# Maxima over the partitions taken by two TensorE products instead of a GpSimd reduction, and a mask and an identity built by VectorE

## The chip, the cores and the metric

The kernel runs on one core of a Trainium2 chip. What counts is the device time of one execution, in microseconds (us). The engines are named as the profile names them: PE is TensorE (PEld its weight loads), DVE is VectorE, ACT is ScalarE, POOL is GpSimd, SP is SyncE, which issues the DMAs. Each engine runs its own instructions in one fixed order; between engines they wait on semaphores.

## The reference

Attention over 2 batches and 8 heads of 576 tokens with 64 features each, then two dense stages over 1152 tokens of 512 features:

```
out_d  = softmax(scale * q_d k_d^T) v_d        # q_d, k_d, v_d: means over 4 neighbouring tokens
attn   = softmax(where(|i - j| < 4, scale * q k^T, -1e9)) v
x      = repeat(out_d, 4) + attn
x      = (silu(x @ w_gate) * (x @ w_val)) @ w_out                 # d_ff 1536
logits = x @ w_gate2;  P = exp(logits - max);  8 rounds of row and column normalization
out    = sum over 8 experts of P[:, e] * (relu(x @ w1[e]) @ w2[e])   # d_ff 1024
```

Inputs and outputs are float32, except that the three weights of the first dense stage come as float64.

## The kernel before, in words

**Three stages.** The attention works on 8 pairs of heads (2 batches, 4 pairs each). For each head `scores` makes the banded products (`s`, with the mask added by a product of the bf16 identity `identb` and the bf16 mask `maskb`) and the pooled ones, DVE takes row maxima (`stm`) and their scaled negatives (`nb`), ACT the exponentials (`ex`), DVE the reciprocal of the sums (`rs`), and POOL multiplies them in. `turn` transposes the result on PE with the float32 identity `ident` (`t`, copied to `at`), `combine` multiplies by v (`o`) and makes x1 from two averages (`x`), which is split into two float16 halves (`xhl`) with one scale for all of x1. POOL also pools q and v (`qt`, `qd`, `vt`, `vdz`). Four heads are started ahead (`AHEAD`).

The first dense stage (MoE 1) multiplies these halves by gate and value weights. `prep_gv(f)` loads a column block f as float64 words (`rawg`), converts it on ACT and DVE (`cvg`, five passes), takes the largest magnitude of each partition (`mxg`), then **the maximum over the partitions**, makes a power of two of it (`pow2`: `u`, `s`, `i`), and splits the block into halves (`gv`). The twelve blocks are numbered 0 to 11; blocks 0 to 4 are prepared while the attention still runs, and the products of blocks 0 to 2 on the first 512 tokens (24 each, in the two PSUM banks of tag `y`) lie between those of the attention. After the attention come the other blocks, w_out, and the second dense stage (MoE 2), 8 experts with Winograd's form of Strassen's products.

**The maximum over the partitions** is `allmax`, used 34 times: once for x1's scale (`g_v`, of a sum of products `vv` of v with itself), 12 times for the gate and value blocks (`g_gv`), twice each for `g_a` and `g_x`, once for the logits (`g_lg`) and 16 times for the experts' weights (`g_w`).

**Order.** A scheduler writes every engine's order from the program text and a timeline of its own; queues then run in that order. Where an instruction waits, everything behind it on its engine waits too.

**Constants.** POOL sets the mask and the identity with its affine_select; ACT makes bf16 copies; DVE clears three halves of `qz` (q of two heads, each padded with zeros), POOL the fourth and the pads of `vz` and `vdz`.

An instruction named ISA in POOL's order stands for a change of the code that POOL has loaded or for a custom instruction; a custom one has an output and an input behind it.

Of the kernel before, what the change touches and what calls it, by code (L numbers as in the profile page):

```python
# [36 lines left out]
HI_MIN = 2.0 ** -15  # L37
NEG = -1.0e9
# [11 lines left out]
NWARM = 5  # L50
QDV = (0, 1, 2)
# [4 lines left out]
def tile_kernel(ctx, tc, qT, kT, vw, vd4, va, wgv, wo, wg2, w1, w2, out):  # L56
    nc = tc.nc
# [18 lines left out]
    # products of zeros while the first loads run, so that the tensor engine's clock is up  # L76
# [10 lines left out]
    V.memset(qz[0][64:, 0], 0.0)  # L87
    V.memset(qz[0][:64, 1], 0.0)
    V.memset(qz[1][64:, 0], 0.0)
# [3 lines left out]
    for i in range(2):  # L93
# [3 lines left out]
    mask = ap.tile([P, P], F32, tag="mask", bufs=1, name="mask")  # L97
    G.memset(mask, 0.0)
    G.affine_select(out=mask, in_=mask, compare_op=ALU.is_ge, fill=NEG, base=FAC - 1,
                    pattern=[[-1, P]], channel_multiplier=1)  # L100
    band = G.affine_select(out=mask, in_=mask, compare_op=ALU.is_ge, fill=NEG, base=FAC - 1,
                    pattern=[[1, P]], channel_multiplier=-1)
    with tc.issue_after(band.ins):
        ident = ap.tile([P, P], F32, tag="ident", bufs=1, name="ident")
        make_identity(nc, ident)
        identb = ap.tile([P, P], BF16, tag="identb", bufs=1, name="identb")
        A.copy(identb, ident)
        maskb = ap.tile([P, 4, P], BF16, tag="maskb", bufs=1, name="maskb")
        A.copy(maskb, mask[:, None, :].to_broadcast([P, 4, P]))
        G.memset(qz[1][:64, 1], 0.0)  # L110
        for i in range(2):
            G.memset(vz[i][:, :, 0, 64:], 0.0)
            G.memset(vz[i][:, :, 1, :64], 0.0)
            G.memset(vdz[i][:, :, 0, 64:], 0.0)
            G.memset(vdz[i][:, :, 1, :64], 0.0)
        ones = cp.tile([P, P], F32, name="ones")
        G.memset(ones, 1.0)
# [20 lines left out]
    def allmax(mx, n, nm):  # L138
        g = tmp(n, f"g_{nm}")
        G.partition_all_reduce(g, mx, channels=P, reduce_op=RED.max)  # L140
        return g
# [41 lines left out]
    def prep_gv(f):  # L183
        """A column block of w_gate and of w_val."""
        w = wp.tile([P, 7 * 4 * P], F16, tag="wA", bufs=WB, name=f"gv{f}")
        w = w[:, :4 * DM].rearrange("p (a n) -> p a n", a=2)
        src = load_f64(wgv[f], f"g{f}", f >= NX)
        mx = tmp(1, f"mxg{f}")
        A.activation(w[:, 0], src, AF.Abs, accum_out=mx)
        s, gv_inv[f] = pow2(allmax(mx, 1, f"gv{f}"), 1, f"gv{f}")  # L190
        split(w[:, 0], w[:, 1], src, s)
        gv_w[f] = w
# [4 lines left out]
    def prep_wo(i):  # L197
        """Two row blocks of w_out, each row with its own scale."""
# [13 lines left out]
    def prep_w1(e):  # L212
        """The left operands of the seven products, of one column block of each half at a time."""
        r = []
# [7 lines left out]
        m = tmp(1, f"mw1{e}")  # L222
        V.tensor_reduce(m, allmax(mx, 4, f"w1{e}"), axis=AX.X, op=ALU.max)
        s, inv = pow2(m, 1, f"w1{e}", room=4.0)
# [25 lines left out]
    def prep_w2(e):  # L250
# [10 lines left out]
        m = tmp(1, f"mw2{e}")  # L261
        V.tensor_reduce(m, allmax(mx, 4, f"w2{e}"), axis=AX.X, op=ALU.max)
        s, inv = pow2(m, 1, f"w2{e}")
# [37 lines left out]
    def x1_scale():  # L301
        """x1 is the sum of two averages of v, whose largest square lies below the largest entry of a sum of
        Gram matrices; the high halves of the words of v are bfloat16s, close enough for a bound."""
# [10 lines left out]
        V.tensor_scalar(m.bitcast(U32), allmax(mx, 1, "v").bitcast(U32), 0x7F800000, 1, op0=ALU.bitwise_and,  # L314
# [4 lines left out]
    def attention():  # L319
        """Generator: the pieces of the attention, of two heads at a time."""  # L320
# [153 lines left out]
    def gv_step(c, f, early):  # L474
# [17 lines left out]
        if early:  # L492
            # silu(g) = g (1 + tanh(g / 2)) / 2, in the table that holds exp
# [28 lines left out]
    ia = {}  # L522

    def act_split(c):
# [3 lines left out]
        g = allmax(sc, KF1, f"a{c}")  # L528
        m = tmp(1, f"ma{c}")
        V.tensor_reduce(m, g, axis=AX.X, op=ALU.max)  # L530
        s, ia[c] = pow2(m, 1, f"a{c}")
# [16 lines left out]
    def w_out(c):  # L548
        """x2, its part of the routing's logits, and the right operands of the seven products."""
# [46 lines left out]
    def routing():  # L596
# [4 lines left out]
        g = allmax(m, 1, "lg")  # L601
        V.tensor_scalar(g, g, -1.0, None, op0=ALU.mult)
# [68 lines left out]
    def h_step(e, c, between=None):  # L671
        """relu(w1^T x2) by Winograd's form of Strassen's seven products, on halves of rows, columns and k."""
# [141 lines left out]
```

## Time and profile before

| | |
|---|---|
| time of the kernel, median of 3 runs | 1090.13 us (1089.25 to 1091.47) |
| span of the profiled execution, first to last instruction | 1088.1 us |
| PE busy | 1022.6 us (94%) |
| DVE busy | 763.4 us (70%) |
| ACT busy | 449.8 us (41%) |
| POOL busy | 96.7 us (9%) |
| DMA moved | 67.92 MB, 62 GB/s on average |

The page gives the profiled execution's time only as its span; the median of the runs lies 2.0 us above that span, and a sum made on the span is carried over to the median by that difference. A busy time is a share of the whole span; what a wait costs is read from the stage in which it lies. "issue" as a releaser means that the profile shows nothing that the engine waited for.

### The profile page before, as it was taken

The page shows a single profiled execution, that of the slowest core. Times are in us where ns is not written, and L with a number is a line of the kernel's source. Part 1 is how long each engine was busy: PE and PEld are TensorE (multiplying, and loading weights), DVE is VectorE, ACT ScalarE, POOL GpSimd, SP SyncE. Part 2 cuts the span into 40 slices and gives each one's busy share as a digit, 9 for nine tenths or more (in the row PEclk, how much of TensorE's full clock was granted, in tenths as well). Part 3 has the DMA queues.
Part 4 walks back from the last instruction along what each step waited for, and adds up shares of the span by engine and source line. Part 5 has one row for each costly group of instructions (what it writes and reads, how often), then busy time and mean ns, then how long its engine had stood idle before and what let it go on. Part 6 is the DMA issues. An engine that isn't in the chain of part 4 may idle for free.

```text
span 1088.1 us, 16397 instructions
## 1 busy us (share of the span) xinstructions
PE 1022.6 (94%) x6493; PEld 657.3 (60%) x6493; DVE 763.4 (70%) x1557; ACT 449.8 (41%) x933; POOL 96.7 (9%) x147
## 2 busy tenths in 40 slices
PE   5756677999999999999999999999999999999998
PEld 4745455566656776656666565575665665666654
DVE  5835565788768299979758866984974974985631
ACT  4654364666646073723414422621541441351210
POOL 3634440000000020000000000000000000000000
PEclk9977888999999999999999999999999999999999
DMA  7721222243202002210301201211111030120001
GB/s 200 243 68 33 85 91 78 86 147 116 79 1 78 1 2 78 78 42 37 117 1 39 86 31 39 78 40 39 65 52 33 8 117 1 40 78 1 1 35 53
DMA packets 23613, 67.92 MB, mean 62 GB/s; under 512 B 12208, under 2 KB 12464, under 8 KB 17136
## 3 DMA queue, kind: packets, MB, share of 16 engines
q1 hardware_dynamic: 23536, 66.87, 18.2%
q8 instruction: 51, 0.84, 0.3%
q14 instruction: 26, 0.21, 0.1%
HBM read 64.50 MB, written 2.36 MB: 61 GB/s over the span
## 4 chain that ended last, share of the span: by engine, by line
PE 83%; DVE 6%; issue 6%; POOL 2%; ACT 2%; POOLq 0%; ACTq 0%; DVEq 0%
PE y L155 34%; PE p L155 29%; PE gv L155 9%; PE wo L155 6%; PE o L425 1%; PE lgps L546 1%; PE s L355 1%; PE s L361 0%; DVE nb L370 0%; DVE cvg L174 0%; ACT ex L373 0%; POOL ex L384 0%; DVE gv L148 0%; DVE stm L365 0%; POOL g_gv L140 0%
## 5 line engine op out<-in xcount | busy, mean ns | idle before, releaser
L155 PE MATMUL y<-w,hhl 128*128 128x512 f16 (+1 forms) x1752 | 396.2, 376 | 0.0
L155 PE MATMUL p<-bop,w 128*128 128x320 f16 (+1 forms) x2688 | 353.8, 286 | 0.8 <-DVE u L685 0.7
L155 PEld LDWEIGHTS <-w 128*128 128x128 f16 x2688 | 263.0, 98 | 90.5 <-issue 1.3
L155 PEld LDWEIGHTS <-hhl 128*128 128x128 f16 x1752 | 171.5, 98 | 178.0
L155 PE MATMUL gv<-xhl,gv 128*128 128x320 f16 (+1 forms) x864 | 148.9, 333 | 5.7 <-DVE act L504 4.0
L713 ACT ACTIVATE hhl<-h 128x640 f16<-128x640 f32 (+1 forms) x128 | 83.1, 676 | 169.0 <-DVE h L685 169.0
L155 PEld LDWEIGHTS <-gv 128*128 128x128 f16 x864 | 85.5, 99 | 63.1 <-issue 12.5
L744 DVE SCALAR_TENSOR_TENSOR acc<-y,pe,acc 128x512 f32<-128x512 f32 (+1 forms) x64 | 47.3, 739 | 101.3 <-PE y L155 100.5
L147 ACT ACTIVATE w<-r,s_w 128x256 f16<-128x256 f32 (+1 forms) x96 | 71.0, 783 | 110.2 <-PE y L155 86.3
L714 DVE SCALAR_TENSOR_TENSOR hhl<-h,hhl 128x640 f16<-128x640 f32 (+1 forms) x128 | 94.3, 753 | 15.9 <-ACT hhl L713 14.7
L685 DVE SCALAR_TENSOR_TENSOR h<-p,u 128x256 f32<-128x256 f32 (+1 forms) x192 | 84.8, 452 | 19.0 <-PE p L155 13.3
L148 DVE SCALAR_TENSOR_TENSOR w<-r,s_w,w 128x256 f16<-128x256 f32 (+1 forms) x96 | 78.2, 833 | 16.7 <-ACT w L147 16.7
L155 PE MATMUL wo<-ahl,wo 128*128 128x320 f16 (+1 forms) x432 | 71.5, 326 | 0.0
L685 DVE SCALAR_TENSOR_TENSOR u<-p,u 128x320 f32<-128x320 f32 (+1 forms) x128 | 57.3, 448 | 4.8 <-PE p L155 4.1
L147 ACT ACTIVATE w<-cmb,s_w 128x512 f16<-128x512 f32 x64 | 43.0, 710 | 41.1 <-DVE cmb L238 38.9
L155 PEld LDWEIGHTS <-wo 128*128 128x128 f16 x432 | 42.3, 99 | 26.9
L140 POOL PARTITION_ALL_REDUCE g_w<-mxw x16 | 7.3, 458 | 567.1 <-DVE mxw L136 331.8
L702 ACT ACTIVATE s<-p 128x256 f32<-128x256 f32 (+1 forms) x64 | 25.4, 397 | 53.3 <-PE p L155 53.3
L136 DVE TENSOR_REDUCE mxw<-r 128x1 f32<-128x1024 f32 x32 | 37.5, 1213 | 14.1 <-DMA r<-in_w 14.1
L148 DVE SCALAR_TENSOR_TENSOR w<-cmb,s_w,w 128x512 f16<-128x512 f32 x64 | 45.9, 741 | 0.0
L258 ACT ACTIVATE j<-r 128x1024 f16<-128x1024 f32 x32 | 33.4, 1046 | 25.4 <-DMA r<-in_w 25.4
L373 ACT ACTIVATE ex<-s,nb 128x128 f32<-128x128 f32 x64 | 22.6, 372 | 24.7 <-DVE nb L367 24.2
(192 smaller groups left out, 956.2 us busy)
## 6 DMA issues: line engine op xcount, KB each, us to landing
r<-in_w SPq DMA_DIRECT2D x32, 1024.0 KB, 4.8
rawg<-in_wgv SPq DMA_DIRECT2D x12, 1024.0 KB, 5.1
rawo<-in_wo SPq DMA_DIRECT2D x6, 1024.0 KB, 4.9
vz<-in_vw SPq DMA_DIRECT2D x16, 160.0 KB, 4.6
k<-in_kT SPq DMA_DIRECT2D x8, 288.0 KB, 6.7
qz<-in_qT SPq DMA_DIRECT2D x16, 144.0 KB, 4.0
v<-in_vd SPq DMA_DIRECT2D x8, 288.0 KB
va<-in_va SPq DMA_DIRECT2D x8, 288.0 KB, 7.9
```

The lines of the kernel that those rows point to most:

```text
L136: V.tensor_reduce(o, i, axis=axis, op=ALU.max, apply_absolute_value=True)
L147: return (A.activation(hi, src, AF.Copy, scale=s), V.scalar_tensor_tensor(lo, src, s, hi, op0=ALU.mult, op1=ALU.subtract))
L148: V.scalar_tensor_tensor(lo, src, s, hi, op0=ALU.mult, op1=ALU.subtract))
L155: T.matmul(ps, lhsT=wf(i, k), rhs=xf(j, k), start=n == 0, stop=n == 3 * nk - 1)
L258: A.activation(junk, t[:, 2 * j:2 * j + 2].rearrange("p a n -> p (a n)"), AF.Abs, accum_out=mx[:, 2 * i + j:2 * i + j + 1])
L355: T.matmul(ps[0][:, w * P:(w + 1) * P], lhsT=q[:, j, ws], rhs=k[:, ws], start=False, stop=w == NW - 2)
L373: A.activation(ex[:, 0, w * P:(w + 1) * P], ps[0][:, w * P:(w + 1) * P], AF.Exp, scale=0.125, bias=nb[:, w:w + 1], accum_out=sm[:, w:w + 1])
L685: V.scalar_tensor_tensor(o, ps, HSC, u, op0=ALU.mult, op1=ALU.add)
L702: A.activation(s1, p1, AF.Copy, scale=HSC)
L713: ra = A.activation(t[:, 0], h, AF.Relu)
L714: rv = V.scalar_tensor_tensor(t[:, 1], h, 0.0, t[:, 0], op0=ALU.max, op1=ALU.subtract)
L744: V.scalar_tensor_tensor(acc[t][:, ds], ps, p[:, t:t + 1], acc[t][:, ds], op0=ALU.mult, op1=ALU.add)
```

## The change

Each maximum over partitions is first reduced to one value a partition where there are several (that reduction stood behind the maximum before). For x1's scale and for the blocks 0 to 5 of `prep_gv`, seven maxima, PE then multiplies the column by the identity, which lays it out as a row in PSUM, DVE takes the row's maximum, and PE spreads that to all partitions by a product with a row of ones. The others stay with POOL. Mask and identity are built by DVE from the squared distance of row and column, and `ident` is kept for the whole program; POOL clears all of `qz`. Comments were removed, too, so line numbers shift (the helper `mm3` is at L172 after, at L155 before; `allmax` is at L143 to L158 after).

```diff
+NSHORT = 6
...
-    V.memset(qz[0][64:, 0], 0.0)
-    V.memset(qz[0][:64, 1], 0.0)
-    V.memset(qz[1][64:, 0], 0.0)
+    for i in range(2):
+        G.memset(qz[i][64:, 0], 0.0)
+        G.memset(qz[i][:64, 1], 0.0)
...
-    mask = ap.tile([P, P], F32, tag="mask", bufs=1, name="mask")
-    G.memset(mask, 0.0)
-    G.affine_select(out=mask, in_=mask, compare_op=ALU.is_ge, fill=NEG, base=FAC - 1,
-                    pattern=[[-1, P]], channel_multiplier=1)
-    band = G.affine_select(out=mask, in_=mask, compare_op=ALU.is_ge, fill=NEG, base=FAC - 1,
-                    pattern=[[1, P]], channel_multiplier=-1)
-    with tc.issue_after(band.ins):
-        ident = ap.tile([P, P], F32, tag="ident", bufs=1, name="ident")
-        make_identity(nc, ident)
-        identb = ap.tile([P, P], BF16, tag="identb", bufs=1, name="identb")
-        A.copy(identb, ident)
-        maskb = ap.tile([P, 4, P], BF16, tag="maskb", bufs=1, name="maskb")
-        A.copy(maskb, mask[:, None, :].to_broadcast([P, 4, P]))
...
+    dist = ap.tile([P, P], F32, tag="dist", bufs=1, name="dist")
+    V.memset(dist[:, 0:1], 0.0)
+    for n in (1, 2, 4, 8, 16, 32, 64):
+        V.tensor_scalar(dist[:, n:2 * n], dist[:, :n], float(n), None, op0=ALU.add)
+    row = ap.tile([P, 32], F32, tag="row", bufs=1, name="row")
+    V.transpose(row, dist[:, :32])
+    for n in range(32, P, 32):
+        V.tensor_scalar(row[n:n + 32, 0:1], row[n:n + 32, 0:1], float(n), None, op0=ALU.add)
+    V.tensor_scalar(dist, dist, row[:, 0:1], None, op0=ALU.subtract)
+    V.tensor_tensor(dist, dist, dist, op=ALU.mult)
+    identb = ap.tile([P, P], BF16, tag="identb", bufs=1, name="identb")
+    V.tensor_scalar(identb, dist, 0.0, None, op0=ALU.is_equal)
+    maskb = ap.tile([P, 4, P], BF16, tag="maskb", bufs=1, name="maskb")
+    V.tensor_scalar(maskb, dist[:, None, :].to_broadcast([P, 4, P]), FAC * FAC - 0.5, NEG,
+                    op0=ALU.is_ge, op1=ALU.mult)
+    ident = cp.tile([P, P], F32, name="ident")
+    V.tensor_scalar(ident, dist, 0.0, None, op0=ALU.is_equal)
...
-    def allmax(mx, n, nm):
-        g = tmp(n, f"g_{nm}")
-        G.partition_all_reduce(g, mx, channels=P, reduce_op=RED.max)
-        return g
+    def allmax(mx, n, nm, short=False):
+
+        if n > 1:
+            m = tmp(1, f"gm_{nm}")
+            V.tensor_reduce(m, mx, axis=AX.X, op=ALU.max)
+            mx = m
+        if not short:
+            g = tmp(1, f"g_{nm}")
+            G.partition_all_reduce(g, mx, channels=P, reduce_op=RED.max)
+            return g
+        ps = psg.tile([P, 512], F32, tag="y", name=f"sm_{nm}")
+        r = tmp(1, f"gr_{nm}")
+        T.matmul(ps[:1, :P], lhsT=mx, rhs=ident, start=True, stop=True)
+        V.tensor_reduce(r[:1], ps[:1, :P], axis=AX.X, op=ALU.max)
+        T.matmul(ps[:, P:P + 1], lhsT=ones[:1], rhs=r[:1], start=True, stop=True)
+        return ps[:, P:P + 1]
...
-        s, gv_inv[f] = pow2(allmax(mx, 1, f"gv{f}"), 1, f"gv{f}")
+        s, gv_inv[f] = pow2(allmax(mx, 1, f"gv{f}", f < NSHORT), 1, f"gv{f}")
```

The change moves instructions on every engine. On POOL, before, in the middle of the attention, around the maximum of block 1 (`ex` is the scaling of the exponentials):

```order
L384 TENSOR_TENSOR ex_740<-ex_740,rs_748 128x512
L386 TENSOR_SCALAR ex_740<-ex_740,rs_748 128x128
L388 TENSOR_TENSOR ex_740<-ex_740,rs_748 72x288
L140 ISA
L140 ISA g_gv_769<-mxg_767 128x1
L334 ISA
L334 TENSOR_TENSOR qd_961<-qt_964 128x288
L341 TENSOR_TENSOR vt_1071<-v_939 72x256
L342 TENSOR_TENSOR vt_1071<-v_939 72x256
```

and at the same place after (the scaling stands at L397 to L401, the pooling of q at L346 and L347, that of v at L354 to L358):

```order
L358 TENSOR_TENSOR vdz_85<-vt_955 72x2x64
L346 TENSOR_TENSOR qt_978<-qz_81 128x576
L347 TENSOR_TENSOR qd_975<-qt_978 128x288
L358 TENSOR_TENSOR vdz_85<-vt_955 72x2x64
L354 TENSOR_TENSOR vt_1085<-v_953 72x256
L355 TENSOR_TENSOR vt_1085<-v_953 72x256
L397 TENSOR_TENSOR ex_705<-ex_705,rs_713 128x512
```

Before, six such changes of code with a maximum between them stand among POOL's work of the attention; after, there is none from the first `vt` to the last `ex`. One stands ahead of the first `vt`, behind the memsets; the next is behind the last `ex`, ahead of `g_gv` of block 6. Those around the four `bop` subtractions of MoE 1's end are there before and after.

On PE, after, the two products of block 1's maximum (`sm_gv`) lie around a transposed head and the scores of another:

```order
L374 MATMUL s_1_689<-kd_683,qd_682 72x144 x2
L155 MATMUL sm_gv_780<-ident,mxg_778 1x128
L410 MATMUL t_0_719<-ident,ex_458 128x128 x4
L411 MATMUL t_1_720<-ident,ex_458 128x128
L414 MATMUL t_1_720<-ident,ex_458 72x72 x4
L365 LDWEIGHTS identb
L365 MATMUL s_0_734<-maskb,identb 128x512
L368 MATMUL s_0_734<-k_472,qz_81 128x128 x4
L370 LDWEIGHTS identb
L370 MATMUL s_1_735<-maskb,identb 128x128
L372 MATMUL s_1_735<-k_472,qz_81 128x128
L374 MATMUL s_1_735<-kd_683,qd_682 72x144 x2
L157 MATMUL sm_gv_780<-gr_gv_781,ones 128x1
```

They are new on PE; before, nothing of a maximum stood there. The first waits for ACT (`mxg`), the second for DVE (`gr_gv`).

At the beginning of DVE's order, before (`kd` and `qd` pool k and q of the first two pairs, `stm` are the first row maxima):

```order
L330 TENSOR_REDUCE kd_169<-k_136 128x144
L336 TENSOR_REDUCE qd_168<-qz_81 128x288
L330 TENSOR_REDUCE kd_299<-k_140 128x144
L336 TENSOR_REDUCE qd_298<-qz_82 128x288
L365 TENSOR_REDUCE stm_87<-s_0_172 128x4
```

and after, where the doubling of `dist` has begun ahead of the first row here:

```order
L343 TENSOR_REDUCE kd_174<-k_141 128x144
L109 TENSOR_SCALAR dist<-dist 128x32
L111 STREAM_TRANSPOSE row<-dist 128x32
L349 TENSOR_REDUCE qd_173<-qz_81 128x288
L109 TENSOR_SCALAR dist<-dist 128x64
L113 TENSOR_SCALAR row<-row 32x1 x3
L343 TENSOR_REDUCE kd_307<-k_145 128x144
L114 TENSOR_SCALAR dist<-dist,row 128x128
L349 TENSOR_REDUCE qd_306<-qz_82 128x288
L115 TENSOR_TENSOR dist<-dist 128x128
L117 TENSOR_SCALAR identb<-dist 128x128
L119 TENSOR_SCALAR maskb<-dist 128x512
```

The chain that gives `identb` and `maskb` now stands on DVE, and its last part behind the pooling of the second pair's q.

## Rows read from the trace of the kernel before

**Rows 1.** The page's second part: the span in 40 slices of 27.2 us; busy tenths of PE, and the granted clock of TensorE in tenths of full speed.

```profile
PE   5756677999999999999999999999999999999998
PEclk9977888999999999999999999999999999999999
```

**Rows 2.** Busy time of the engines in four stretches: stretch, its length, then us busy (instructions) of PE, PEld, DVE, ACT and POOL, the granted clock, the DMA engines' share and GB/s.

```profile
3.30:13.50 10.20, 0.19 (x1) 0.00 (x0) 4.25 (x10) 0.91 (x2) 3.06 (x12) 1.00 1.08 254
13.50:176.30 162.80, 112.91 (x737) 93.41 (x738) 96.95 (x214) 84.05 (x317) 72.24 (x99) 0.83 0.33 102
176.30:300.00 123.70, 123.37 (x780) 76.09 (x778) 97.51 (x179) 79.59 (x141) 5.19 (x8) 1.00 0.32 111
400.00:1088.00 688.00, 684.54 (x4277) 418.41 (x4275) 495.35 (x1008) 237.10 (x399) 8.68 (x17) 1.00 0.13 47
```

**Rows 3.** POOL's instructions in order of time: start, duration, what, and in brackets the idle time before it with what ended that. The instructions between two gaps are left out.

```profile
52.28 0.38 POOL L140 PARTITION_ALL_REDUCE g_v<-mxv  x1 [6.34 <-issue]
61.37 1.14 POOL L333 TENSOR_TENSOR qt<-qz 128x576 f32<-128x576 f32 x1 [8.71 <-issue]
...
76.36 0.38 POOL L140 PARTITION_ALL_REDUCE g_gv<-mxg  x1 [5.97 <-issue]
83.58 0.65 POOL L334 TENSOR_TENSOR qd<-qt 128x288 f32<-128x288 f32 x1 [6.84 <-issue]
...
98.85 0.38 POOL L140 PARTITION_ALL_REDUCE g_gv<-mxg  x1 [5.95 <-issue]
106.26 0.89 POOL L334 TENSOR_TENSOR qd<-qt 128x288 f32<-128x288 f32 x1 [7.03 <-issue]
...
121.88 0.38 POOL L140 PARTITION_ALL_REDUCE g_gv<-mxg  x1 [6.71 <-issue]
129.16 1.03 POOL L384 TENSOR_TENSOR ex<-ex,rs 128x512 f32<-128x512 f32 x1 [6.91 <-issue]
...
149.35 0.38 POOL L140 PARTITION_ALL_REDUCE g_gv<-mxg  x1 [7.26 <-issue]
156.55 1.65 POOL L345 TENSOR_TENSOR vdz<-vt 72x128 f32<-72x128 f32 x2 [6.82 <-DVE rs L382]
...
168.13 0.38 POOL L140 PARTITION_ALL_REDUCE g_gv<-mxg  x1 [5.77 <-issue]
```

**Rows 4.** The waits between 40 and 176.3 us: who waited for whom, us in total, times, longest.

```profile
DVE u_gv L129 <- POOL g_gv L140: 35.1, 5, 9.6
ACT ex L373 <- DVE nb L367: 18.9, 5, 8.9
PE s L361 <- POOL qd L334: 16.1, 2, 8.6
```

**Rows 5.** Columns as in rows 2: the sum over the six stretches 45.9 to 61.4, 70.4 to 83.6, 92.9 to 106.3, 115.2 to 129.2, 142.1 to 156.6 and 162.4 to 176.3 us.

```profile
sum 84.50, PE 45.04 PEld 36.10 DVE 39.59 ACT 40.65 POOL 2.49; mean PE 7.51 PEld 6.02 DVE 6.60 ACT 6.77 POOL 0.41
```

**Rows 6.** Columns as in rows 2: three stretches without such a gap, and their sum.

```profile
26.00:40.00 14.00, 13.77 (x128) 12.72 (x127) 13.03 (x25) 12.31 (x54) 12.84 (x19) 1.00 1.00 313
104.00:117.00 13.00, 11.54 (x76) 9.02 (x76) 8.65 (x14) 7.09 (x24) 8.83 (x12) 0.86 0.44 140
126.00:143.00 17.00, 16.65 (x97) 11.57 (x96) 13.65 (x21) 10.17 (x33) 12.86 (x13) 0.83 0.07 16
sum 44.00, PE 41.96 PEld 33.31 DVE 35.33 ACT 29.57 POOL 34.53; mean PE 13.99 PEld 11.10 DVE 11.78 ACT 9.86 POOL 11.51
```

**Rows 7.** The beginning, in order of time, columns as in rows 3.

```profile
7.39 0.74 DVE L330 TENSOR_REDUCE kd<-k 128x144 f32<-128x576 f32 x1
...
10.37 0.28 POOL L99 TENSOR_SCALAR_AFFINE_SELECT mask<-mask 128x128 f32<-128x128 f32 x1 [9.45 <-issue]
...
11.05 0.62 ACT L109 CAST maskb<-mask 128x512 bf16<-128x512 f32 x1 [9.05 <-POOL mask L101]
...
11.71 1.35 DVE L336 TENSOR_REDUCE qd<-qz 128x288 f32<-128x1152 f32 x1 [3.58 <-POOL qz L110]
...
13.52 0.61 PE L352 MATMUL s<-maskb,identb 128*128 128x512 bf16 x1 [10.03 <-ACT identb L107]
```

**Rows 8.** PE in order of time: one head's scores from the first row to the second, a pair's `combine` from the second to the third, a head's `turn` from the third to the fourth; ten products `vv`; eight of a gate block; the last products of the attention.

```profile
29.38 0.38 PE L352 MATMUL s<-maskb,identb 128*128 128x512 bf16 x1
...
31.34 0.76 PE L417 MATMUL o<-at,vdz 72*128 72x144 f32 x4
...
34.63 0.60 PE L397 MATMUL t<-ident,ex 128*128 128x128 f32 x4
...
35.42 1.14 PE L309 MATMUL vv<-va 128*128 128x128 bf16 x10
...
88.08 1.90 PE L155 MATMUL gv<-xhl,gv 128*128 128x512 f16 x8
...
174.62 1.69 PE L425 MATMUL o<-at,vz 128*128 128x120 f32 x8
```

**Rows 9.** Two single rows: a DVE maximum over a row of 128 values, and a transposing PE product of 128 columns in float32.

```profile
42.90 0.28 DVE L312 TENSOR_REDUCE mxv<-vv 128x1 f32<-128x128 f32 x1
...
26.25 0.27 PE L398 MATMUL t<-ident,ex 128*128 128x128 f32 x1
```

**Rows 10.** DVE in order of time: the same small product of 128 by 4 values at two places.

```profile
66.51 2.95 DVE L370 TENSOR_TENSOR nb<-stm,scl 128x4 f32<-128x4 f32 x1
...
70.93 0.15 DVE L367 TENSOR_TENSOR nb<-stm,scl 128x4 f32<-128x4 f32 x1
```

More of the change, by code (lines that the diff above doesn't have):

```diff
@@ L6 @@
 from concourse._compat import with_exitstack
-from concourse.masks import make_identity
 F32 = mybir.dt.float32
@@ L95, in tile_kernel @@
         V.memset(sts[i], 1.0)
-    mask = ap.tile([P, P], F32, tag="mask", bufs=1, name="mask")
-    G.memset(mask, 0.0)
-    G.affine_select(out=mask, in_=mask, compare_op=ALU.is_ge, fill=NEG, base=FAC - 1,
-                    pattern=[[-1, P]], channel_multiplier=1)
-    band = G.affine_select(out=mask, in_=mask, compare_op=ALU.is_ge, fill=NEG, base=FAC - 1,
-                    pattern=[[1, P]], channel_multiplier=-1)
-    with tc.issue_after(band.ins):
-        ident = ap.tile([P, P], F32, tag="ident", bufs=1, name="ident")
-        make_identity(nc, ident)
-        identb = ap.tile([P, P], BF16, tag="identb", bufs=1, name="identb")
-        A.copy(identb, ident)
-        maskb = ap.tile([P, 4, P], BF16, tag="maskb", bufs=1, name="maskb")
-        A.copy(maskb, mask[:, None, :].to_broadcast([P, 4, P]))
[L110 to L117, printed above, removed]
+    for i in range(2):
+        G.memset(vz[i][:, :, 0, 64:], 0.0)
+        G.memset(vz[i][:, :, 1, :64], 0.0)
+        G.memset(vdz[i][:, :, 0, 64:], 0.0)
+        G.memset(vdz[i][:, :, 1, :64], 0.0)
@@ new lines, in tile_kernel @@
+    ones = cp.tile([P, P], F32, name="ones")
+    G.memset(ones, 1.0)
+    dist = ap.tile([P, P], F32, tag="dist", bufs=1, name="dist")
[6 more added lines that the diff above has]
+        V.tensor_scalar(row[n:n + 32, 0:1], row[n:n + 32, 0:1], float(n), None, op0=ALU.add)
@@ L221, in prep_w1 @@
             r.append(t)
-        m = tmp(1, f"mw1{e}")
-        V.tensor_reduce(m, allmax(mx, 4, f"w1{e}"), axis=AX.X, op=ALU.max)
-        s, inv = pow2(m, 1, f"w1{e}", room=4.0)
+        s, inv = pow2(allmax(mx, 4, f"w1{e}"), 1, f"w1{e}", room=4.0)
         a = []
@@ L260, in prep_w2 @@
             r.append(t)
-        m = tmp(1, f"mw2{e}")
-        V.tensor_reduce(m, allmax(mx, 4, f"w2{e}"), axis=AX.X, op=ALU.max)
-        s, inv = pow2(m, 1, f"w2{e}")
+        s, inv = pow2(allmax(mx, 4, f"w2{e}"), 1, f"w2{e}")
         b = []
@@ L313, in x1_scale @@
         m = tmp(1, "mv")
-        V.tensor_scalar(m.bitcast(U32), allmax(mx, 1, "v").bitcast(U32), 0x7F800000, 1, op0=ALU.bitwise_and,
+        V.tensor_scalar(m.bitcast(U32), allmax(mx, 1, "v", True).bitcast(U32), 0x7F800000, 1, op0=ALU.bitwise_and,
                         op1=ALU.logical_shift_right)
@@ L527, in act_split @@
         V.tensor_tensor(sc, amx[c], wo_inv, op=ALU.mult)
[L528 to L531, printed above, removed]
+        s, ia[c] = pow2(allmax(sc, KF1, f"a{c}"), 1, f"a{c}")
         V.tensor_scalar(sc, wo_inv, s, None, op0=ALU.mult)
@@ L570, in operands @@
         pool = m2 if c else mp
-        m = tmp(1, f"m2{c}")
-        V.tensor_reduce(m, allmax(mx, KD, f"x2{c}"), axis=AX.X, op=ALU.max)
-        s, ix2[c] = pow2(m, 1, f"x2{c}", room=4.0)
+        s, ix2[c] = pow2(allmax(mx, KD, f"x2{c}"), 1, f"x2{c}", room=4.0)
         w = xp.tile([P, 7, 2, 2, nh], F16, tag=f"bop{c}", name=f"bop{c}")
@@ L600, in routing @@
         V.tensor_reduce(m, lg, axis=AX.XY, op=ALU.max)
-        g = allmax(m, 1, "lg")
-        V.tensor_scalar(g, g, -1.0, None, op0=ALU.mult)
+        g = tmp(1, "lgn")
+        V.tensor_scalar(g, allmax(m, 1, "lg"), -1.0, None, op0=ALU.mult)
         A.activation(prob, lg, AF.Exp, bias=g)
```

## The prediction

> **What bounds the kernel now.** I read the slices first. PE is at 9 tenths from the eighth slice to the last but one; only in the first seven, to about 190 us, is it at 5 to 7 [rows 1]. By stretches: from 176.3 us, where the last products of the attention end [rows 8], to 300 us PE is busy 123.4 of 123.7 us, and from 400 us on 684.5 of 688.0 [rows 2]. So all behind the attention is bound by PE, and whatever the attention's end moves by, the end of the program moves by, as long as the blocks' preparation keeps up. In the attention, 13.5 to 176.3 us, no engine is the bound: PE 112.9 us, DVE 97.0, ACT 84.1, POOL 72.2 of 162.8, at a mean granted clock of 0.83, which between the levels 1.2 and 2.4 GHz means that a third of that time lies at the lower one [rows 2].
>
> What is the bound there, then? POOL's order in time shows it. Around each maximum of 0.38 us POOL stands still twice, 5.8 to 7.3 us before it and 6.8 to 8.7 behind it, for nothing that the profile shows ("issue") [rows 3]. In the program's order these are the places where the code is changed. The last gap behind is put down to a DVE reciprocal, but its length is that of the others. The eleven gaps sum to 74.3 us (6.34 + 8.71 + 5.97 + 6.84 + 5.95 + 7.03 + 6.71 + 6.91 + 7.26 + 6.82 + 5.77).
>
> Who pays: DVE waits 35.1 us with `u_gv` for the maximum, with the row maxima and reciprocals of the next heads queued behind it; ACT 18.9 us for the scaled negatives that DVE then brings late; PE 16.1 us for the pooled q that POOL brings late [rows 4]. In the six stretches that hold the gaps, 84.5 us, PE works 45.0 us, DVE 39.6, POOL 2.5 [rows 5]. Outside them, in three stretches, PE is at 95% (42.0 of 44.0), DVE at 80% (35.3), POOL at 78% [rows 6]. The attention runs in bursts, with one halt for each maximum.
>
> **The change part by part.**
>
> *Seven maxima leave POOL.* With them go all changes of code in the attention: in the new order there is none between the first `vt` and the last `ex`. All eleven gaps go; the load of code ahead of the first `vt` stays, its nearest price being the 9.45 us ahead of the first affine_select [rows 7]. It comes after POOL's memsets, now some 4 us, so `vt` starts at about 14 us as before, and the first combine needs it much later. The next change of code follows the last `ex`, beside PE's products of MoE 1, and block 6 is only needed after three more blocks.
>
> *What the seven cost instead.* DVE: a maximum over one row of 128, 0.28 us [rows 9], seven times, 2.0 us. PE: two products; the first moves 128 columns in float32, 0.27 us [rows 9], the second one column, which no row shows: between nothing and the same 0.27. I take 0.27 twice, 3.8 us in all. They also hold one of the two banks of tag `y`, which in the attention only the gate products of blocks 0 to 2 share. The waits are the larger matter, since the second product waits on PE for DVE, with everything of PE behind it; the order puts a turn and a head's scores between the two, 0.79 and 1.96 us at full clock [rows 8]. Cover of 2.75 us for a DVE maximum of 0.28: I take nothing, and leave the other case to the rivals.
>
> *The beginning.* The first scores start at 13.52 us behind `identb`, and that behind POOL's load of code [rows 7]. After, DVE builds `dist` in between its pooling. The pooling of the second q now waits for its DMA and no longer for POOL's clearing: before it waited 3.58 us for that [rows 7], and could have started at 8.13 (11.71 less 3.58, the end of `kd`). Then 1.35 us of pooling, some 0.2 for the last subtraction, 0.3 each for the square and `identb` (bound above by the 0.28 of a row of the same 128 columns [rows 9]) and 0.62 for `maskb` as on ACT [rows 7]: 10.8 us, or 9.9 if the small ones cost nothing. I take 10.5 us: 3.0 us sooner. The doublings before them lie in DVE's idle time (busy 4.25 of 10.2 us before 13.5 [rows 2]).
>
> *The attention without halts.* What is left is a pipeline through four engines; the longest is now DVE with 97.0 us and 2.0 more, 99.0. PE's floor at full clock: 8 pairs of two scores, two turns and a combine, 2 x 1.96 + 2 x 0.79 + 3.29 = 8.8 us each, from the starts in [rows 8], 70.3; 40 products `vv` in four lots of at most 1.14, 4.6; 72 gate products at most at 0.24 (1.90 / 8), 17.1; the seven maxima 3.8. That is 95.8 us instead of 112.9 + 3.8, since short waits should keep the clock up. Both are bounds that a pipeline doesn't reach. Its pace is best read from the stretches without gaps: DVE busy 93, 67 and 80% of the time, 80% together [rows 6]. 99.0 / 0.80 = 123.3 us; from 10.5 us the stage ends at 133.8, where it ended at 176.3: 42.5 us sooner. At 93% the end is at 117.0 (59.3 sooner), at 67% at 158.3 (18.0 sooner).
>
> *What is late next.* Blocks 5 and on are prepared by DVE while PE multiplies; there DVE was busy 97.5 of 123.7 us [rows 2], 79%, so a backlog is worked off only slowly. In the new order the conversion of block 5 stands behind the attention's last `xhl`. DVE's 99.0 us above still hold it, so I take nothing for it; if PE outruns it, PE halts once for some us.
>
> The rest is moved work of one price: a maximum over one to twelve values now stands ahead of POOL's and not behind it. From MoE 2 on PE's order is the same but for names.
>
> Sum on the profiled span: 1088.1 - 42.5 = 1045.6 us; with the 2.0 us by which the median of the runs lies above that span, 1047.6. I say **1047 us**.
>
> The Trainium skill speaks against the change: GPSIMD Engine Reference, "When to use GPSIMD", counts cross-partition reduction among the things that only GpSimd can do, and VectorE: DVE Perf Modes, "Why `tensor_reduce` can't reduce along partition axis", sends such reductions there. By that rule the seven should stay where they are and the time with them, 1090 us. The trace agrees that the reduction itself is cheap on POOL, 0.38 us; what it shows besides is the halt of 12 to 15 us around it [rows 3], which the rule doesn't weigh, and the way around it goes through TensorE.
>
> **The rivals.**
>
> *PE becomes the bound, nearly all is won back.* For it: PE at 98% in two of the three stretches without gaps [rows 6]. The stage then ends between PE's floor, 10.5 + 95.8 = 106.3 us (70.0 sooner, 1020 us), and DVE at 88%, 10.5 + 112.5 = 123.0 (53.3 sooner, 1037). Against it: these stretches worked off what a halt had piled up, and all four engines must keep pace.
>
> *POOL and DVE hinder each other more.* A product of 128 by 4 values takes DVE 0.15 us at one place and 2.95 at another, at which POOL had just begun to work again [rows 10]. POOL's 72 us would lie in 123 us instead of 163, so such stretches become a third more frequent; DVE then runs at 72% or less of its present work: 99.0 / 0.72 = 137.5 us, end at 148.0, 28.3 sooner, 1062 us, up to the 1072 of the 67% stretch, and with a halt of up to 13 us behind the attention for blocks 5 and 6, 1085. The Trainium skill has the cause in GPSIMD Engine Reference, "Specifications": GpSimd's ways to SBUF are shared with VectorE, with contention from some kinds of VectorE instructions. The pair of rows agrees with it.
>
> *The small products halt PE; slower.* PE comes to the second product of a maximum while DVE is still far behind, since DVE's order has conversions and row maxima ahead of `gr`. It decides where PE waits 42.5 / 7 = 6.1 us each time: DVE must be 8.9 us late beyond the 2.75 of cover at each of the seven. One wait of 9.6 us of this kind stands in the profile [rows 4], but that was POOL's halt itself. At 7 us each it is 6.3 us slower, 1096.
>
> *It does nothing.* The halts would have to be hidden: then PE would be nearly full in the stretches that hold them, and it works 45.0 of 84.5 us there [rows 5]. 1090 us.
>
> **How the numbers follow.** Pace between 72 and 88%, 1037 to 1062 us: 0.58; PE-bound, 1020 to 1037: 0.16; hindered or short of blocks, 1062 to 1085: 0.18; no change: 0.03; slower: 0.05. The range leaves out the outer parts of both tails, about 0.05 below 1028 and 0.15 above 1068. A difference of over 0.2%, 2.2 us, can be told from none here: faster 0.92, same 0.03, slower 0.05.
>
> **What would show it.** POOL without idle "issue" gaps from its first `vt` to the last `ex`; the first `s` at about 10.5 us; the last product `o` near 134 us; DVE at 75 to 85% in between; a granted clock near 1.00 there; PE full from then on. I am wrong if PE waits long ahead of `sm_gv`'s second product or of `t` and `o` for DVE, if `identb` comes late, or if PE halts between 134 and 180 us for blocks 4 to 6.

## The result, and the profile after

The changed kernel takes 1053.65 us (median of 4 runs, 1052.66 to 1055.02) where the kernel before takes 1089.85 us: a ratio of 0.9674, 95% interval 0.9654 to 0.9693. The profiled span fell from 1088.1 to 1053.2 us, by 34.9. Forecast were 1047 us and a span 42.5 us shorter.

The page's slices, to be held against [rows 1], and four stretches of the changed kernel, columns as in [rows 2] (the attention's last product `o` ends at 127.3 us):

```profile
PE   6787998999999999999999999999999999999998
PEclk9899899999999999999999999999999999999999
```

```profile
10.70:127.30 116.60, 101.14 (x732) 88.30 (x733) 87.75 (x205) 81.19 (x312) 72.17 (x90) 0.91 0.50 141
127.30:180.00 52.70, 47.24 (x263) 25.49 (x262) 38.83 (x71) 29.19 (x47) 0.73 (x2) 0.97 0.28 100
180.00:300.00 120.00, 119.82 (x729) 71.53 (x728) 95.97 (x174) 74.67 (x129) 3.65 (x7) 1.00 0.23 80
400.00:1053.00 653.00, 649.92 (x4057) 396.81 (x4055) 460.67 (x923) 220.47 (x372) 4.55 (x13) 1.00 0.13 46
```

The attention is now a stretch of 116.6 us with PE at 87%. New is a loss behind it: from 127.3 to 180 us PE does nothing for 5.5 us. All of the change lies ahead of MoE 1's second half. Its first products, those of w_out, before and after:

```profile
301.82 15.70 PE L155 MATMUL wo<-ahl,wo 128*128 128x512 f16 x72
266.89 12.90 PE L172 MATMUL wo<-ahl,wo 128*128 128x512 f16 x59
```

They stand 786.3 us from the end in both (and in every kernel below, within 0.4).

The beginning, in order of time, columns as in [rows 7]; then PE's first combine:

```profile
8.51 1.35 DVE L349 TENSOR_REDUCE qd<-qz 128x288 f32<-128x1152 f32 x1
...
10.23 0.42 DVE L119 TENSOR_SCALAR maskb<-dist 128x512 bf16<-128x512 f32 x1
...
10.71 0.59 PE L365 MATMUL s<-maskb,identb 128*128 128x512 bf16 x1 [7.22 <-DMA vz<-in_vw]
...
12.87 0.71 POOL L354 TENSOR_TENSOR vt<-v 72x256 f32<-72x256 f32 x1 [7.72 <-issue]
...
14.38 1.28 ACT L386 ACT_TABLE_LOAD   x1 [14.38 <-DVE nb L380]
15.67 0.37 ACT L386 ACTIVATE ex<-s,nb 128x128 f32<-128x128 f32 x1
...
20.70 1.15 ACT L193 ACTIVATE cvg<-rawg 128x1024 f32<-128x1024 f32 x1
...
33.21 0.72 POOL L354 TENSOR_TENSOR vt<-v 72x256 f32<-72x256 f32 x1 [5.05 <-DMA v<-in_vd]
...
38.89 1.33 PE L430 MATMUL o<-at,vdz 72*128 72x144 f32 x4 [4.74 <-ACT ex L386]
```

The first scores start at 10.71 us, 2.8 sooner, behind DVE's `maskb`, which ends at 10.65 (the row puts the wait down to a DMA; in e10 the same row names `maskb`). But the first combine, at 31.34 us before [rows 8], now stands at 38.89. Three things have slipped in between: a load of ACT's function table (1.28 us) between the first scores and the first exponential, the conversion `cvg` of blocks 0 and 1 among the first heads' exponentials, and a wait of 5.05 us for `v`.

Behind the attention, PE, DVE, ACT and POOL in order of time:

```profile
127.09 5.34 PE L172 MATMUL gv<-xhl,gv 128*128 128x512 f16 x24
...
151.06 0.38 PE L155 MATMUL sm_gv<-ident,mxg 128*1 128x128 f32 x2
151.37 3.71 PE L172 MATMUL gv<-xhl,gv 128*128 128x320 f16 x26
155.00 0.38 PE L157 MATMUL sm_gv<-gr_gv,ones 1*128 1x1 f32 x2
...
155.42 0.16 DVE L134 TENSOR_SCALAR u_gv<-sm_gv 128x1 f32<-128x1 f32 x1 [3.25 <-PE sm_gv L157]
...
159.24 1.16 ACT L190 ACTIVATE cvg<-rawg 128x1024 f32<-128x1024 f32 x1
...
170.38 0.38 POOL L151 PARTITION_ALL_REDUCE g_gv<-mxg  x1 [54.93 <-ACT gv L206]
...
174.76 1.04 PE L172 MATMUL gv<-xhl,gv 128*128 128x512 f16 x4 [4.05 <-ACT gv L164]
```

The 24 gate products at 127.09 us complete the 72 that before lay ahead of the last `o`: equal work ends at 132.4 us instead of 176.3, **43.9 us sooner**. Then the two small products of block 5 stand 26 gate products apart in a full queue; DVE, which needed the answer at 152.2 us, gets it at 155.4; block 6 starts its conversion at 159.2, and PE stops for 4.05 us. Between 132.4 us and w_out **9.0 us are given back**: that stretch lasts 134.5 us, and 125.5 before. Of this, PE stands still for 5.6 us instead of 0.3; the other 3.7 are a longer busy time, at a mean granted clock of 0.99 instead of 1.00, with the four small products, 1.5 us, among it.

### The profile page after: what moved, and what is told of

It reads as the page before. It is cut to its first block, busy times and chain, and to the rows that moved or that the text cites. A ratio compares the mean times of both kernels' runs of the same rounds, so it can differ in the third digit from the quotient of the medians.

```text
span 1053.2 us, 16460 instructions
## 1 busy us (share of the span) xinstructions
PE 1019.6 (97%) x6520; PEld 655.2 (62%) x6521; DVE 767.7 (73%) x1578; ACT 450.1 (43%) x931; POOL 94.3 (9%) x138
## 4 chain that ended last, share of the span: by engine, by line
PE 86%; DVE 6%; ACT 3%; DMA 2%; issue 2%; SPq 0%; POOL 0%; ACTq 0%; DVEq 0%
PE y L172 35%; PE p L172 30%; PE gv L172 8%; PE wo L172 7%; DMA k<-in_kT 2%; PE o L438 2%; ACT ex L386 1%; PE o L430 1%; DVE cvg L196 1%; PE s L368 1%; PE lgps L556 1%; DVE cvg L191 1%; DVE cvg L195 0%; PE t L410 0%; DVE act L528 0%
## 5 line engine op out<-in xcount | busy, mean ns | idle before, releaser
L172 PE MATMUL y<-w,hhl 128*128 128x512 f16 (+1 forms) x1752 | 396.2, 376 | 0.0
L172 PE MATMUL p<-bop,w 128*128 128x320 f16 (+1 forms) x2688 | 354.6, 286 | 0.8 <-DVE u L693 0.7
L172 PEld LDWEIGHTS <-w 128*128 128x128 f16 x2688 | 263.0, 98 | 90.8 <-issue 1.5
L172 PEld LDWEIGHTS <-hhl 128*128 128x128 f16 x1752 | 171.4, 98 | 178.2
L172 PE MATMUL gv<-xhl,gv 128*128 128x320 f16 (+1 forms) x864 | 145.5, 328 | 6.5 <-ACT gv L164 4.1
L172 PEld LDWEIGHTS <-gv 128*128 128x128 f16 x864 | 84.2, 98 | 62.8 <-issue 5.6
L164 ACT ACTIVATE w<-r,s_w 128x256 f16<-128x256 f32 (+1 forms) x96 | 71.1, 783 | 115.2 <-PE y L172 86.3
L172 PE MATMUL wo<-ahl,wo 128*128 128x320 f16 (+1 forms) x432 | 71.5, 326 | 0.0
L172 PEld LDWEIGHTS <-wo 128*128 128x128 f16 x432 | 42.3, 99 | 26.9
L151 POOL PARTITION_ALL_REDUCE g_w<-gm_w x16 | 5.9, 372 | 569.1 <-DVE gm_w L147 563.2
L141 DVE TENSOR_REDUCE mxw<-r 128x1 f32<-128x1024 f32 x32 | 37.5, 1213 | 12.6 <-DMA r<-in_w 12.6
L273 ACT ACTIVATE j<-r 128x1024 f16<-128x1024 f32 x32 | 33.4, 1045 | 26.0 <-DMA r<-in_w 26.0
L693 DVE SCALAR_TENSOR_TENSOR u<-p,s 128x256 f32<-128x256 f32 (+1 forms) x64 | 28.8, 451 | 5.2 <-PE p L172 3.9
```

The costliest lines, as they stand in the source:

```text
L141: V.tensor_reduce(o, i, axis=axis, op=ALU.max, apply_absolute_value=True)
L164: return (A.activation(hi, src, AF.Copy, scale=s), V.scalar_tensor_tensor(lo, src, s, hi, op0=ALU.mult, op1=ALU.subtract))
L273: A.activation(junk, t[:, 2 * j:2 * j + 2].rearrange("p a n -> p (a n)"), AF.Abs, accum_out=mx[:, 2 * i + j:2 * i + j + 1])
L693: V.scalar_tensor_tensor(o, ps, HSC, u, op0=ALU.mult, op1=ALU.add)
```

## The experiments

Each kernel's time is given as its ratio to the kernel before, run on the same chip beside it, with the 95% interval; 0.001 is 1.1 us. A profiled execution can lie some us beside its kernel's median (e3: a span of 1050.8, a median of 1054.93), so times go by the ratios and places by the traces.

| kernel | ratio | interval | median us |
|---|---|---|---|
| changed | 0.9674 | 0.9654 to 0.9693 | 1053.65 |
| e1 new constants alone | 1.0058 | 1.0045 to 1.0071 | 1095.10 |
| e2 short maxima alone | 0.9656 | 0.9643 to 0.9670 | 1051.55 |
| e3 one maximum back to POOL | 0.9701 | 0.9683 to 0.9719 | 1054.93 |
| e4 `NSHORT` 4 | 0.9593 | 0.9580 to 0.9606 | 1044.37 |
| e5 two loads held back | 0.9674 | 0.9658 to 0.9690 | 1053.55 |
| e6 old constants, `NSHORT` 4 | 0.9536 | 0.9523 to 0.9549 | 1038.37 |
| e7 = e4 and e5 | 0.9598 | 0.9585 to 0.9611 | 1044.91 |
| e8 `NSHORT` 12 | 0.9745 | 0.9729 to 0.9760 | 1060.82 |
| e9 = e4, table load first | 0.9584 | 0.9571 to 0.9597 | 1043.86 |
| e10 = e9, conversions later | 0.9552 | 0.9539 to 0.9565 | 1040.94 |
| e11 = e10, order of loads too | 0.9572 | 0.9559 to 0.9585 | 1042.92 |
| e12 = e4 and e3 | 0.9606 | 0.9588 to 0.9623 | 1045.90 |

### The two halves of the change: e1, e2

e1, beside `allmax(mx, 1, "v")` without its last argument:

```diff
-NSHORT = 6
+NSHORT = 0
```

> The changed kernel with all maxima over the partitions left to GpSimd; mask and identity by VectorE, as changed. If the terms of the sum add up, only the earlier start is left of the change, 3.0 us (2.8 as the trace of after has it): 1087.0 us, a ratio of 0.9973, with POOL's idle gaps of 6 to 9 us around each maximum still there. Rival: the attention is paced by those gaps, and what starts 3 us sooner waits at the first of them: 1090 us. Rival on the other side: the gain lay in the constants, since POOL's queue is cleared of them: below 1070 us.

e2 takes back `dist` and its followers, the affine_select, make_identity, copies and clearing as before:

> The changed kernel with mask and identity built as before (affine_select on POOL, casts on ACT) and the seven maxima by TensorE. If the terms add up: 1053.65 + 2.8 = 1056.5 us, first score at 13.5 us, no idle gap without a cause on POOL from the first vt to the last ex. Rival: a start 3 us later is absorbed by the waits for DMA (k at 35 us, v at 33 us) and for blocks 5 and 6 after the attention: 1053.5 to 1054.5 us.

The new constants alone make the kernel **slower, by 6.3 us**; the maxima alone give 37.5 us, as much as both together. All three guesses on e1 missed, though its first score does come at 10.7 us; on e2 the rival is nearer, but it had not reckoned with a gain, and the first score came at 12.09 us, not at 13.5: beside short maxima the new constants start the scores only 1.4 us sooner. So the gain is the maxima's. In e2 the last products `o` start at 115.25 us, in the changed kernel at 126.01, but the loss behind the attention stays: PE stops for 2.00 us at 121 and for 4.05 at 166.

### The small products in a full queue: e4, e8

```diff
-NSHORT = 6
+NSHORT = 4
```

> The changed kernel with the maxima of blocks 4 and 5 also by GpSimd; both stand behind the last ex in POOL's order, so the attention keeps no code change. Theory A: blocks 5 and 6 come late because the two small products stand in order in a full PE queue, 24 to 26 products apart, and VectorE waits 2.72 and 3.25 us for the second one; then these waits and PE's hole of 4.05 us go: 1045 to 1050 us. Theory B: VectorE's and ScalarE's conversions are simply behind since the attention ended sooner; the hole stays, only its releaser changes: 1053 to 1055 us. Theory C: the code change for the first GpSimd maximum is on the path: 1056 to 1062 us.

> The changed kernel with all twelve blocks' maxima by TensorE. If a pair of small products in a full PE queue delays its block by 3 to 6 us each time, as blocks 4 and 5 suggest (4 us of hole and some 8 us of time for two of them), six more of them bring further holes between 170 and 260 us: 4 us for each of at least three blocks, 1065 us or more. If the loss of 9 us was blocks 5 and 6 alone, out of step once after a fast attention: 1052 to 1056 us.

e4 confirms theory A: 8.8 us less than the changed kernel. PE, ACT and POOL of e4 behind the attention:

```profile
125.29 9.66 PE L172 MATMUL gv<-xhl,gv 128*128 128x512 f16 x44
135.16 44.49 PE L172 MATMUL gv<-xhl,gv 128*128 128x320 f16 x276 [0.21 <-ACT act L527]
...
143.13 0.35 POOL L151 PARTITION_ALL_REDUCE g_gv<-mxg  x1 [13.42 <-ACT gv L206]
...
147.71 1.14 ACT L190 ACTIVATE cvg<-rawg 128x1024 f32<-128x1024 f32 x1
```

Block 5's maximum is through at 143.5 us, block 6's conversion starts at 147.7 instead of 159.2, and PE multiplies 276 times in one piece. POOL has nothing else to do there: it starts the maximum at 143.13 us, 0.1 us behind ACT, which makes its input until 143.03, so the change of code holds up nothing. e8 went the other way as theory A has it, though less far than its 1065 us: 7.7 us slower than the changed kernel. Its PE row:

```profile
167.78 0.38 PE L155 MATMUL sm_gv<-ident,mxg 128*1 128x128 f32 x2
169.09 0.38 PE L157 MATMUL sm_gv<-gr_gv,ones 1*128 1x1 f32 x2 [0.93 <-DVE gr_gv L156]
170.80 0.38 PE L155 MATMUL sm_gv<-ident,mxg 128*1 128x128 f32 x2 [1.34 <-ACT gv L206]
171.55 0.38 PE L157 MATMUL sm_gv<-gr_gv,ones 1*128 1x1 f32 x2 [0.37 <-DVE gr_gv L156]
```

Here the other danger shows: where the gate products have run out, the chain of product, maximum, product itself holds PE.

### What one halt of POOL costs: e3, e12

```diff
-        s, gv_inv[f] = pow2(allmax(mx, 1, f"gv{f}", f < NSHORT), 1, f"gv{f}")
+        s, gv_inv[f] = pow2(allmax(mx, 1, f"gv{f}", f < NSHORT and f != 1), 1, f"gv{f}")
```

> The changed kernel with the maximum of block 1 alone given back to GpSimd, in the middle of the attention: one pair of code changes, 12 to 14 us of idle POOL. If the time goes by the sum of the gaps, one pair of 5.5 costs 42.5 / 5.5 = 7.7 us: 1061 us. If a single halt is on the path in full: 1053.65 + 13 = 1066 us. If a single one is covered by the heads started ahead, or by what the stage behind the attention gives back anyway: 1054 to 1056 us.

> e4 with the maximum of block 1 given back to GpSimd in the middle of the attention (as e3, but now without the late blocks that could hide it). If e3's 1 to 2 us was the true price of one pair of code changes, because four heads are started ahead: 1045 to 1047 us. If the blocks that came late hid it: 1044.4 + 7.7 = 1052 us, or with all of the 14 us on the path 1058 us.

One pair costs 2.9 us in e3 and 1.4 us in e12, neither told with certainty from nothing (the intervals overlap). But all of them, e1 against the changed kernel, cost 0.0384, 41.8 us, for 73.2 us of gaps: 7.6 us a pair. Against e4, which like e1 leaves blocks 4 and 5 to POOL, it is 0.0465, 50.6 us, 9.2 a pair. POOL of e12 around its one pair, then the same two stretches of e12 and of e4, which has no such pair, columns as in [rows 2]:

```profile
66.97 0.38 POOL L151 PARTITION_ALL_REDUCE g_gv<-mxg  x1 [6.65 <-DMA qz<-in_qT]
74.00 1.64 POOL L397 TENSOR_TENSOR ex<-ex,rs 128x512 f32<-128x512 f32 x1 [6.65 <-DVE rs L395]
```

```profile
60.00:80.00 20.00, 13.43 (x84) 10.79 (x84) 13.34 (x37) 13.64 (x52) 6.54 (x10) 0.83 0.35 107
80.00:100.00 20.00, 20.00 (x164) 17.77 (x163) 14.41 (x37) 16.26 (x66) 18.21 (x26) 1.00 0.33 80
...
60.00:80.00 20.00, 20.00 (x150) 17.62 (x149) 16.71 (x41) 17.41 (x72) 13.37 (x16) 0.92 0.60 156
80.00:100.00 20.00, 16.64 (x132) 14.17 (x130) 18.18 (x38) 13.18 (x46) 16.90 (x21) 1.00 0.17 44
```

The two gaps of e12 are put down to a DMA and to DVE, but they have the length of the others. The halt takes 6.6 us of PE's time in its stretch; in the next 20 us, with PE without a break and POOL at 91%, e12 wins half of that back against e4 (33.4 us of PE's work in the 40, and 36.6 in e4). That suggests reading the halts as POOL's work. From its first `vt` to its last `ex` POOL was taken, gaps included, for 71.5 + 68.5 = 140.0 of 148.7 us before, 94%; in e12 for 71.4 + 13.3 = 84.7 of 102.1, 83%; in the changed kernel for 72.2 of 102.6, 70%. By this reading one halt finds room in POOL's slack, and where one comes every 23 us there is hardly any left. The reading is argued from these shares; no run varies them by themselves, and the number of pairs at which it turns was not measured.

### Why the constants cost: e5, e6, e7, e9, e10, e11

e6 is e2 with `NSHORT = 4`, the best of all, 4.6% faster than the kernel before. Against e4 it differs in the constants alone, and these cost 0.0057, 6.2 us. Its first score stands at 11.81 us, 1.1 behind e4's, but its first combine at 29.57. ACT and PE of e6:

```profile
0.72 1.28 ACT L110 ACT_TABLE_LOAD   x1 [0.72 <-PEq L807]
...
29.57 0.76 PE L426 MATMUL o<-at,vdz 72*128 72x144 f32 x4
...
31.37 1.20 ACT L189 ACTIVATE cvg<-rawg 128x1024 f32<-128x1024 f32 x1
```

Suspected first was the order of loads. With the new constants the DMA queue has both 1 MB loads `rawg` of blocks 0 and 1 ahead of `k` and `qz` of the third pair, before behind them. e5 holds them back, e7 is e5 with `NSHORT = 4`:

```diff
         if n in PREP_AT:
-            prep_gv(PREP_AT.index(n))
+            with tc.issue_after(pair_in[2].ins):   # the last load of q of the third pair
+                prep_gv(PREP_AT.index(n))
```

> The changed kernel, with the loads of gate blocks 0 and 1 (1 MB each) held back in the order of the DMA queue until q and k of the third pair are issued, as they stood before the change. If these two loads are why the new constants gain nothing: POOL's wait of 5.05 us for v and VectorE's of 2.10 us for k go, the attention's last product o comes 4 us or more sooner than the 127.3 us of the changed kernel, and the time falls by the 1.5 to 4.5 us that lie between the changed kernel and maxima alone with the earlier start added: 1048 to 1051.5 us. Rival: VectorE's own work on the constants (7.06 of 7.20 us busy at the start) is the price: 1053 us, no change.

> Mask and identity as before, maxima of x1 and of blocks 0 to 3 by TensorE, the others by GpSimd: experiments e2 and e4 together. If the late blocks behind the attention were what kept e2's sooner attention (its last o at 116.95 us, with 12 gate products fewer done, against 127.3 us) from counting: 1044.4 less the 7.5 us of equal work, 1037 us. If the conversions on VectorE and ScalarE are the next bound: 1042 to 1045 us, with holes in PE's row between 120 and 180 us.

> The changed kernel with the two block loads held back (as e5) and the maxima of blocks 4 and 5 by GpSimd (as e4). By the first theory of e6 with the start of 10.7 us instead of 12.1: 1036 us; by the second 1042 to 1045 us.

e6 comes near the first theory (1037 us), e5 and e7 gain nothing against the changed kernel and e4. In e5 the wait of 5.05 us for `v` is down to 2.52 (another of 3.12 us stands at 17.94), the longest wait of DVE for `k` is 4.4 us instead of 2.1, and the first combine stands at 33.6 us, but from 40 to 60 us PE works 12.61 us instead of 19.66, with waits of 3.66 us for `x` and 2.10 for `ex`; what in the new order makes these late was not followed. e7 has the time of the second theory, but not its holes: from 120 to 180 us its PE is full, and the loss lies in the attention.

So the load order alone is not it. e9 puts the table load first; e10 also moves ACT's and DVE's conversions of blocks 0 and 1 behind the second head's `at`; e11 forces loads and x1's products as well:

```diff
+    tab = ap.tile([P, 1], F32, tag="tab", bufs=1, name="tab")
+    A.activation(tab, scl[:, :1], AF.Exp)
...
-            prep_gv(PREP_AT.index(n))
+            with tc.issue_after(mark[1].ins):      # the last copy of at of head 1
+                prep_gv(PREP_AT.index(n))
```

> e4 (maxima of blocks 4 and 5 by GpSimd too) with one exponential of a single column put on ScalarE at the start, so that the table load of 1.28 us, which stands at 14.4 us between the first scores and the first exponential since ScalarE makes no copies of the constants any more, lies ahead of them as before the change. If that load sits on the path: 1044.4 - 1.3 = 1043.1 us. If later waits absorb it: 1044.4 us.

> e9 with the conversions of gate blocks 0 and 1 put behind the second head's transposed copies, as their place was before the change (there from 31.4 us, in the changed kernel from 20.7 us); the order of the loads stays that of the changed kernel. If the conversions, in order ahead of the exponentials and reciprocals of the first heads on ScalarE and VectorE, are why the new constants cost 6 us (e6 against e4): 1037 to 1040 us, first combine at 30 to 33 us instead of 37. If the early loads are the reason, through late v and k: 1042 to 1044 us.

> New constants, table load early, and by forced order the loads of blocks 0 and 1, their conversions, the second half of the products for x1's scale and its loads about where the order of e6 has them; maxima as in e6. If only the order that came with the new constants cost the time: 1038.4 less the 1.0 us of earlier start, 1037 us. If building the constants on VectorE costs by itself: 1043 us or more.

e9 is 1.0 us faster than e4, a little less than the load's 1.28 and not told from nothing; its first combine, at 39.2 us, comes no sooner than e4's at 37.0. e10 is 3.5 us faster than e9. POOL's third pooling of `v` in e9, then POOL, ACT and PE of e10:

```profile
34.58 0.72 POOL L356 TENSOR_TENSOR vt<-v 72x256 f32<-72x256 f32 x1 [7.11 <-DMA v<-in_vd]
...
34.98 0.73 POOL L357 TENSOR_TENSOR vt<-v 72x256 f32<-72x256 f32 x1 [2.14 <-DMA v<-in_vd]
32.76 2.20 ACT L195 ACTIVATE cvg<-rawg 128x1024 f32<-128x1024 f32 x2
35.12 0.71 PE L433 MATMUL o<-at,vdz 72*128 72x144 f32 x4
```

`cvg` starts at 32.8 us, and the first combine comes at 35.1 instead of 39.2, though `v` lands no sooner. So it is not the late `v`; what is left is the place of the conversions, which e10 forces, with whatever the scheduler moved along with them. That is the larger part of the 6.2 us. e11 shows no further gain (2.2 us more than e10, intervals overlapping). What is left between e10 and e6 (1.7 us, intervals overlapping) stays open.

## Why the prediction was right, and where its terms were not

**POOL's gaps: right.** Between the first `vt` and the last `ex` no gap is left without a cause; the change ahead of the first `vt`, priced at 9.45 by the nearest row, took 7.72 us. The trace of POOL's queue names what stands at the start of the gaps: an instruction `MODIFY_POOL_CONFIG`, before, at 46.1 us ahead of `g_v` and at 52.6, 76.7, 99.2, 122.2 and 149.7 us behind the first five maxima; after, there is one at 5.2 us, ahead of the first `vt`, and the next at 115.7, right behind the last `ex`. The Trainium skill, GPSIMD Engine Reference, "Instruction dispatch", gives about 6 us for the first call of freshly loaded code; the gaps ahead of the reductions agree (5.8 to 7.3 us [rows 3]), those behind them, 6.8 to 8.7, it does not speak of.

**The start: right to 0.2 us and worth less than nothing.** The first scores came at 10.71 us against 10.5 (the terms written there add up to 10.9 and, with the small ones at nothing, to 10.1, not to 10.8 and 9.9; the choice of 10.5 lies between either way). The step that failed is that these 3.0 us would be carried through the attention. The forecast moved DVE's instructions and did not look at what the scheduler does when they move: the blocks' conversions slip ahead of the first heads' work (e10: 3.5 us), and ACT, relieved of its copies, loads its table late (e9: 1.0 us, not told from nothing). With that the constants cost 6.2 us where the maxima are short (e6 against e4) and 6.3 alone (e1), instead of gaining 3.0. In the changed kernel at most 2.0 of it shows (against e2, not told from nothing): where PE has to stop for blocks 5 and 6 anyway, a later end of the attention costs little.

**The attention: right, 43.9 us at equal work against 42.5, but only as a sum, and with luck.** That the halts go, and that a pipeline is left in which no engine is full, is the mechanism that was forecast; that DVE is the one that sets its pace is not shown, PE is busier (87%). DVE ran at 75% (87.75 of 116.6 us; 91.69 of the 121.7 us to equal work), at the lower end of the forecast 75 to 85%, not at 80%, and it did 91.7 us of work to that point, not the 99.0 assumed, since part of the conversion fell behind the attention. The two misses cancel: 99.0 us at 75% would have taken 131.5 us. So do two others. Without the new constants (e2), 72 gate products and all `o` are done at 127.6 us, 48.7 us sooner than before, where the forecast without its 3.0 us of earlier start would have had 39.5: the maxima gave 9.2 us more than forecast, and the constants, put at 3.0 us gained, took 4.8 of that away. The granted clock came up from 0.83 to 0.91, not to 1.00; PE still has waits of 4.74 us (ahead of 38.89) and 4.29 us (ahead of 105.30).

**The small products: right in the attention, wrong behind it.** Taking the waits at nothing held for PE, which waited for none of the fourteen products. But the text looked only at PE waiting for DVE. DVE also waits for PE: once in the attention, 5.89 us at 112.7, with the last heads already scored, and behind it 2.72 and 3.25 us, since a product of one column must stand in line behind 12 and 26 others (the 24 to 26 written for e4 were right for block 5 alone). Each took PE 0.38 us, in two records, instead of 0.27; on seven pairs that is 1.5 us. The rival of this name had its threshold a little off: a wait of 6.1 us each means that DVE is 8.9 us late in all, the 2.75 of cover included, not beyond them.

**What is late next: the term taken as nothing was 9.0 us.** It is the step that parts 1053.65 from 1047: the span fell by 43.9 - 9.0 = 34.9 us instead of 42.5, 7.6 less. The median missed the unrounded 1047.6 us by less than that, 6.05, because the profiled span lies 0.45 us below it and not the 2.0 that were carried over. The text named the place ("if PE halts between 134 and 180 us for blocks 4 to 6") and gave a backlog of DVE as the reason. e4 shows a narrower cause, because the same DVE work with POOL's maximum leaves no hole: the wait of the small products for their turn. The bank of tag `y` that they hold meanwhile is no rival: PE multiplies without a break from 151.06 to 158.9 us. The delay is carried on by the two buffers of `cv`: block 6's first pass starts at 159.24 us, right behind block 5's last read of its own (DVE, 157.93 and 1.28). e4's attention was also done 2.8 us sooner at equal work, so of its 11.4 us on the profiled span 8.6 lie behind it.

**The rivals.** PE-bound: no, 87%. POOL and DVE hindering each other: the pace of 75% is near it, but the end of the stage is not. Small products that halt PE and make it slower: not in the attention; behind it two of the seven cost 8.8 us (e4), and twelve cost 7.7 more than seven (e8). No change, 1090 us, because the reductions belong to POOL: no, though for blocks 4 and 5, where POOL is idle, they do (e4). The halts hidden: six are not; one nearly is (e12), as far as 1.4 us can be told from nothing.

## What to carry to other kernels

As a first estimate, count an engine's halts as its work and compare the sum with the length of the stage: one halt may cost next to nothing and six 40 to 50 us. A short chain over two engines is cheap where its queues have gaps and dear in a full queue, so the slow reduction belongs where its engine is idle, the quick one where the engine is needed. Before an earlier start is counted as a gain, look in the new order at every engine for what has moved into the freed place.

## What was not expected of the hardware

A transposing float32 product of 128 columns and one that spreads a single value each take 0.38 us as two records, so the second is not cheaper for its one column. A DVE maximum over one partition of 128 values takes 0.27 to 0.28 us, as with 128 partitions [rows 9].

ACT's table load is an instruction in its queue, and what comes first behind it decided when it ran. Before, that was a copy, and the load of 1.28 us ran at 0.71 us, 10 us ahead of the copy itself (11.05 us [rows 7]); after, it is the first exponential, and the load waited for DVE's `nb` until 14.38 us. In e9, with a one-column exponential first, it ran at 0.72 us. Why it went ahead of the copy but not of the exponential, no run shows. The Trainium skill, ScalarE: Activation LUTs, "What ACT_TABLE_LOAD costs", gives 1283 ns for it, and more for a drain; the row agrees on the load, and the next activation follows it 0.01 us later, with no drain to be seen here.
